# Local attention's channel sums as one-hot matmuls, and one block of scores a period as powers of e on GpSimd

## The chip, the cores and the metric

The kernel runs on one core of a Trainium2 chip. The metric is the device time of one execution in microseconds (us); of several runs the median counts. Engine names in the profile: PE is TensorE, ACT is ScalarE, DVE is VectorE, POOL is GpSimd, SP is SyncE, which here only issues DMAs.

## What is computed

Two attentions over the same input of 2,048 tokens with 512 channels, 32 heads of 16 channels each, mixed by a gate per token. Cut to what matters:

```python
S, D, H, Dh = 2048, 512, 32, 16
g = sigmoid((x * gate_w).sum(-1, keepdims=True))

# A: full attention
q, k, v = split_heads(x @ A_wqkv)
p = softmax(einsum("bhqd,bhkd->bhqk", q, k) * Dh ** -0.5)
a = merge_heads(einsum("bhqk,bhkd->bhqd", p, v)) @ A_wo

# B: local, dilated attention: 8 keys, at distances 0, 2, ..., 14
q, k, v = split_heads(x @ B_wqkv)
idx = pos[:, None] - 2 * arange(8)[None, :]          # masked where negative
logits = einsum("bhsd,bhswd->bhsw", q, k[idx]) * Dh ** -0.5
o = einsum("bhsw,bhswd->bhsd", softmax(masked(logits)), v[idx])
b = merge_heads(o) @ B_wo

return g * a + (1 - g) * b
```

All inputs and the output are bf16.

## The kernel before

**Full attention.** A *block* is the score tile of one head, 128 keys and 512 queries: 32 heads x 16 key tiles x 4 query chunks = 2,048 blocks. A *period* is one group of four heads (`i`, 0 to 7) with one query chunk (`c_`, 0 to 3); it has 64 blocks, and there are 32 periods, ordered so that two chunks run side by side through the eight groups, then the other two (the change of chunk pair comes after period 16). Four heads sit in four 32-row strips of the array. A block's scores are one matmul (`qk`, line 851), ScalarE turns them into powers of e in sets of three or two blocks (`ex`, line 857: 1,536 or 1,024 columns, tile `pT`, three buffers for each of the two sizes), and a second matmul adds their product with V into the PSUM accumulator `acc` (`pv`, line 870, `pv_mm`, line 818), which has one buffer. A 17th column of ones in V gives the sum of the powers. At a period's end VectorE transposes `acc` (`po1`, line 961, tile `accT`), which frees it for the next period, divides (`po2`) and transposes back (`po3`).

Some of the blocks don't go to ScalarE: in each period `n_dve` blocks (line 20; 3, 2, 4 or 6, in all 116) are done on VectorE by `d_group` (line 888), usually two together. There `dq` makes the scores in a `misc` PSUM tile, `p1` evicts them into `dt`, three scalar_tensor_tensor instructions (`p2`, `p3`, `p4`; tiles `dg` and `pd`, 1,024 wide for two blocks) build the bit pattern of the power, and `pv` multiplies with V. So ScalarE has 1,932 blocks.

**Local attention.** `b_tile` (line 639) runs for each of 16 tiles of 128 tokens. Q, K and V are projected on TensorE in four 32-column strips (`proj`, `mm_ct`, line 250), evicted by VectorE, and K and V written to a scratch in HBM (`kvd`). From there two DMAs load the eight shifted copies of K and V, 1 MB each (`loadk`, `loadv`; tiles `ksh`, `vsh`). GpSimd multiplies K's copies with Q and adds up the 16 channels of each head by halving adds, in two halves of four copies (`logits_half`, line 698). VectorE and ScalarE make the softmax of the 8 logits (`sm_max` to `sm_mul`, lines 723 to 744; `sm_sum` folds 1 - g, `omg`, into 1/sum), GpSimd multiplies with V's copies and adds them (`av_half`, line 749), TensorE transposes the result `obb` (`fin`, line 789) and VectorE puts it into `obt`.

**Output.** For each token tile the output projections of A (`a_mm`) and B (`b_mm`) are done on TensorE, and VectorE mixes them: `a_ev` scales A's by g (`fa`), `b_ev` adds B's (`osb`). The tiles of the last chunk do part of it ahead (`fb_ev`, `fa_ev`, `t_ev`).

**What sets the order.** Every step is an `op` with an engine, an estimated time, a due time, its dependencies, and tokens for the buffers that it takes. `list_schedule` (line 79) simulates these estimates and puts all steps into one order; `Chained` (line 231) and `chain` pin each engine's instructions to it. So each queue is fixed when the program is built, whatever happens on the chip. Where the plan sees TensorE with little to do, it inserts filler matmuls of zeros into `acc` (`zeros`, line 833), which keep TensorE's clock up. Nearly all instructions carry the line of a helper: 239 for `Chained`, 248 for `mm`; lines 422, 616 and 795 are the transpositions of x, of the gate's row, and of `obb`.

The plan's estimate for ScalarE and for the two halves of a tile's logits on GpSimd:

```python
b = op("act", 0.455 * n, ex, tn, deps=[a], alloc=[tp], use=[tr_], name=f"ex{k}")
l0 = opb("pool", 11.9, logits_half(0), tb + 8, deps=[lk, qa], alloc=[tlg], use=[tks, tqb], name=f"lg{t}")
```

Of the kernel before, what the change touches and what calls it, by code (L numbers as in the profile page):

```python
# [20 lines left out]
    dve_tiles=2,  # L21
    b_start=26.0,
# [4 lines left out]
H = 32  # L27
DH = 16
# [6 lines left out]
LN2 = 0.6931471805599453  # L35
SHIFT = 175.0
# [38 lines left out]
WAVE = lambda n: 0.2 + 0.22 * n  # L75
AHEAD = dict(pe=0.10, dve=0.12, act=0.25, pool=0.5, sp=0.0)
# [105 lines left out]
def kernel(  # L182
# [74 lines left out]

    ops = []
# [22 lines left out]
    n_dve = cfg["n_dve"]  # L281
    units, first_unit = [], []
    for pi, (c_, i) in enumerate(periods):
        dset = set(dorder[:n_dve[pi]])
        first_unit.append(len(units))
        units += [(pi, t, j) for t in range(NT) for j in range(4) if (t, j) not in dset]
# [18 lines left out]
    kv_scr = tc.dram_tile([16 + S, 2 * D], BF16, name="kv_scr")  # L305
# [3 lines left out]
    identf = const.tile([NT, NT], FP32, name="identf")  # L309
    ones_t = const.tile([128, QW], BF16, name="ones_t")  # L310
    rowc = const.tile([128, 3], FP32, name="rowc")
    z32 = const.tile([128, 32], BF16, name="z32")
    selq = const.tile([128, 128], BF16, name="selq")
# [13 lines left out]
    def init_warm():  # L327
        V.memset(z32[:], 0.0)
        V.memset(ones_t[:], 1.0)
# [32 lines left out]
    def load_x(sc):  # L362
        def s():
            if sc < 2:
                xl = work.tile([128, W, D], BF16, name="xld", tag="ksh", bufs=2)
            else:
                xl = work.tile([128, NG, QW], BF16, name="xld2", tag="oat", bufs=2)
            SP.dma_start(out=xl[:, 0:TPC, :], in_=x2d[sc * QW:(sc + 1) * QW, :].rearrange("(t p) d -> p t d", p=128))
            xld[sc] = xl
        return s  # L370
# [11 lines left out]
    def load_wo():  # L382
# [4 lines left out]
        SP.dma_start(out=kv_scr[0:16, 0:D], in_=woarr[16:32, 0, :])  # L387
        SP.dma_start(out=kv_scr[0:16, D:2 * D], in_=woarr[16:32, 1, :])

    xtok = [tok("ksh", 2), tok("ksh", 2), tok("oat", 2), tok("oat", 2)]  # L390
# [240 lines left out]
    o_kvd, o_obt = [], []  # L631
    obt_tiles, obt_tok = {}, {}
    WH = W // 2
    HB = D

    def opb(*a, **k):
        return op(*a, cls="b", **k)

    def b_tile(t):
# [3 lines left out]
        rel = max(21.0, tb - 60.0)  # L643

        def proj(key, off, c0):
            def s():
                if c0 == 0:
                    st[key] = misc_ps([128, D])
                    if key == "pk":
                        st["kvs"] = work.tile([128, 2 * D], BF16, name="kvs", tag="kvs", bufs=1)  # L650
                    if key == "pq":
                        st["qb"] = work.tile([128, D], BF16, name="qb", tag="qb", bufs=1)
                for c in range(c0, c0 + 2):
                    mm_ct(st[key], xT[:, c, t * 128:(t + 1) * 128], bw[:, c, off * D:(off + 1) * D], c == 0, c == DC - 1)
            return s
        tkv = tok("kvs", 1)

        def ke():
            V.tensor_copy(out=st["kvs"][:, 0:D], in_=st["pk"][:])

        def ve():
            V.tensor_copy(out=st["kvs"][:, D:2 * D], in_=st["pv"][:])

        def kvd():
            SP.dma_start(out=kv_scr[16 + t * 128:16 + (t + 1) * 128, :], in_=st["kvs"][:])
        tk = tok("misc", 2)
        a = opb("pe", WAVE(2), proj("pk", 1, 0), tb - 14, dense=2, deps=[o_bw] + o_xt[cb], alloc=[tk, tkv], rel=rel)
        a = opb("pe", WAVE(2), proj("pk", 1, 2), tb - 13.5, dense=2, deps=[a], use=[tk])
        ka = opb("dve", 0.71, ke, tb - 13, deps=[a], use=[tk, tkv])
        tk = tok("misc", 2)  # L670
        a = opb("pe", WAVE(2), proj("pv", 2, 0), tb - 12, dense=2, deps=[o_bw] + o_xt[cb], after=[a], alloc=[tk], rel=rel)
        a = opb("pe", WAVE(2), proj("pv", 2, 2), tb - 11.5, dense=2, deps=[a], use=[tk])
        va = opb("dve", 0.71, ve, tb - 11, deps=[a, ka], use=[tk, tkv])
        o_kvd.append(opb("sp", 0.6, kvd, tb - 10, deps=[va], use=[tkv], lat=3.0))

        tqb = tok("qb", 1)

        def qe():
            V.tensor_scalar(out=st["qb"][:], in0=st["pq"][:], scalar1=float(DH) ** -0.5, scalar2=None, op0=ALU.mult)
        tk = tok("misc", 2)  # L680
        a = opb("pe", WAVE(2), proj("pq", 0, 0), tb - 6, dense=2, deps=[o_bw] + o_xt[cb], alloc=[tk, tqb], rel=rel)
        a = opb("pe", WAVE(2), proj("pq", 0, 2), tb - 5.5, dense=2, deps=[a], use=[tk])
        qa = opb("dve", 0.71, qe, tb - 5, deps=[a], use=[tk, tqb])

        def loadk():
            base = kv_scr[16 + t * 128:16 + (t + 1) * 128, :]
            st["ksh"] = work.tile([128, W, D], BF16, name="ksh", tag="ksh", bufs=2)
            SP.dma_start(out=st["ksh"][:], in_=_ap(base, [[2 * D, 128], [-DIL * 2 * D, W], [1, D]]))

        def loadv():  # L690
            st["vsh"] = work.tile([128, W, D], BF16, name="vsh", tag="vsh", bufs=1)
            vbase = kv_scr[16 + t * 128:16 + (t + 1) * 128, D:2 * D]
            SP.dma_start(out=st["vsh"][:], in_=_ap(vbase, [[2 * D, 128], [-DIL * 2 * D, W], [1, D]]))
        tks, tvs, tlg, tob, tbb = tok("ksh", 2), tok("vsh", 1), tok("lg", 2), tok("ob", 1), tok("obb", 1)
        lk = opb("sp", 0.7, loadk, tb - 8, deps=o_kvd[max(0, t - 1):t + 1] + [o_wo], alloc=[tks], lat=10.0)
        lv = opb("sp", 0.7, loadv, tb + 10, deps=o_kvd[max(0, t - 1):t + 1] + [o_wo], alloc=[tvs], lat=9.0)

        def logits_half(hf):
            def s():
                if hf == 0:  # L700
                    st["lg"] = work.tile([128, H, W], FP32, name="lg", tag="lg", bufs=2)
                ksh, lg, qb = st["ksh"], st["lg"], st["qb"]
                prod = work.tile([128, WH, D], FP32, name="prod", tag="prod", bufs=1)
                for w_ in range(WH):
                    for c0 in range(0, D, HB):
                        G.tensor_tensor(out=prod[:, w_, c0:c0 + HB], in0=ksh[:, hf * WH + w_, c0:c0 + HB],
                                        in1=qb[:, c0:c0 + HB], op=ALU.mult)
                pv_ = prod[:].rearrange("p w (h d) -> p w h d", d=DH)
                n = DH
                while n > 2:  # L710
                    n //= 2
                    ws = min(WH, max(1, HB // (H * n)))
                    for w0 in range(0, WH, ws):
                        G.tensor_tensor(out=pv_[:, w0:w0 + ws, :, 0:n], in0=pv_[:, w0:w0 + ws, :, 0:n],
                                        in1=pv_[:, w0:w0 + ws, :, n:2 * n], op=ALU.add)
                G.tensor_tensor(out=lg[:, :, hf * WH:(hf + 1) * WH].rearrange("p h w -> p w h"),
                                in0=pv_[:, :, :, 0], in1=pv_[:, :, :, 1], op=ALU.add)
                if hf == 1 and t * 128 < DIL * (W - 1):
                    G.affine_select(out=lg[:], in_=lg[:], compare_op=ALU.is_ge, fill=NEG,
                                    base=t * 128, pattern=[[0, H], [-DIL, W]], channel_multiplier=1)  # L720
            return s

        def sm_max():
            st["mx"] = work.tile([128, H], FP32, name="mx", tag="mx", bufs=2)
            V.tensor_reduce(out=st["mx"][:], in_=st["lg"][:], axis=AX.X, op=ALU.max)

        def sm_sub():
            lg, mx = st["lg"], st["mx"]
            mx_bc = _ap(mx[:], [list(mx[:].ap[0]), [1, H], [0, W]])
            V.tensor_tensor(out=lg[:], in0=lg[:], in1=mx_bc, op=ALU.subtract)  # L730
# [4 lines left out]
        def sm_sum():  # L735
# [5 lines left out]
            V.tensor_scalar(out=rr[:], in0=rr[:], scalar1=omg[:, t:t + 1], scalar2=None, op0=ALU.mult)  # L741
            st["rr"] = rr

        def sm_mul():
            ex, rr = st["lg"], st["rr"]
            rr_bc = _ap(rr[:], [list(rr[:].ap[0]), [1, H], [0, W]])
            V.tensor_tensor(out=ex[:], in0=ex[:], in1=rr_bc, op=ALU.mult)

        def av_half(hf):
            def s():  # L750
                if hf == 0:
                    st["ob"] = work.tile([128, D], FP32, name="ob", tag="ob", bufs=1)
                else:
                    st["obb"] = work.tile([128, D], BF16, name="obb", tag="obb", bufs=1)
                vsh, attn, ob = st["vsh"], st["lg"], st["ob"]
                prod = work.tile([128, WH, D], FP32, name="prod", tag="prod", bufs=1)
                hn = HB // DH
                for w_ in range(WH):
                    for c0 in range(0, D, HB):
                        a0 = attn[:, c0 // DH:c0 // DH + hn, hf * WH + w_:hf * WH + w_ + 1]  # L760
                        attn_bc = _ap(a0, [list(a0.ap[0]), [W, hn], [0, DH]])
                        G.tensor_tensor(out=prod[:, w_, c0:c0 + HB].rearrange("p (h d) -> p h d", d=DH),
                                        in0=vsh[:, hf * WH + w_, c0:c0 + HB].rearrange("p (h d) -> p h d", d=DH),
                                        in1=attn_bc, op=ALU.mult)
                for c0 in range(0, D, HB):
# [358 lines left out]
```

## Time and profile before

| | |
|---|---|
| three runs | 930.05, 941.4, 946.99 us; median 941.4 |
| the profiled execution | 933.24 us, of it the span 931.5 us |
| granted TensorE clock, mean | 0.984 of full speed |
| first and last exponential of full attention | 21.3 and 919.4 us from the span's start |
| filler matmuls (`acc<-ones_t,z`) | 271 |
| DMA | 47.39 MB, of it 16 MB `ksh` and 16 MB `vsh` |

Times in the page are microseconds from the first to the last instruction of one profiled execution. A row names the line, the engine, the operation, the tile written and the tiles read, their shapes, and the count; behind the bar stand the busy time, the mean of one in ns, and the idle time of the engine just before, with the releaser that ended most of it. Matmuls overlap, so their mean is longer than the pace at which they follow each other.

Stages, busy us of each engine in each (TensorE, its weight loads, VectorE, ScalarE, GpSimd), then the granted clock:

```
20.00:120.00 100.00, 91.70 (x957) 31.38 (x953) 78.89 (x108) 98.00 (x89) 65.08 (x52) 1.00 0.22 65
320.00:420.00 100.00, 90.08 (x899) 30.90 (x897) 78.91 (x104) 99.32 (x90) 92.02 (x73) 1.00 0.17 49
480.00:560.00 80.00, 71.68 (x707) 21.87 (x708) 52.27 (x67) 72.66 (x66) 62.80 (x51) 0.91 0.16 52
560.00:680.00 120.00, 104.83 (x906) 33.32 (x905) 100.50 (x108) 119.75 (x108) 117.03 (x82) 1.00 0.18 51
860.00:919.00 59.00, 50.91 (x492) 16.53 (x488) 43.45 (x53) 56.43 (x51) 0.00 (x0) 1.00 0.02 6
```

### The profile page before, as it was taken

Reading aid. Unit: us, or ns where it says so; the run is one execution under the profiler, and the core shown is the slowest. Engines: PE = TensorE matmul, PEld = TensorE weight load, DVE = VectorE, ACT = ScalarE, POOL = GpSimd, SP = SyncE. Lnnn points to the kernel's source line nnn. Section 1 sums busy time; section 2 is a strip of 40 time slices with the busy share of each in tenths; the row PEclk is TensorE's granted clock in tenths of the full one; section 3 lists DMA queues with packets and bytes.
Section 4 is the critical chain, followed back from the end, with each engine's and each line's share of the span. In section 5 each row is a group of like instructions: output and inputs, shape, how many; then the busy total and the mean of one; then the engine's idle time right before and its main releaser. Section 6 shows DMA issues by size and latency. Waiting matters only on the chain.

```text
span 931.5 us, 18744 instructions
## 1 busy us (share of the span) xinstructions
PE 818.5 (88%) x7720; PEld 271.4 (29%) x7720; DVE 688.0 (74%) x873; ACT 890.5 (96%) x799; POOL 703.4 (76%) x540
## 2 busy tenths in 40 slices
PE   7999998889999989988899899888888788889887
PEld 4223232223332223322223223222222222222222
DVE  4687967858787787886336777988778667876776
ACT  4999998999999999999998989999999999999994
POOL 2357969797999699979893999999999989920000
PEclk9999999999999999999999979999999999899999
DMA  9301210303030211031301020130330100100001
GB/s 272 104 2 58 60 44 1 103 1 103 1 104 13 91 58 46 6 99 57 109 20 62 22 88 12 46 103 1 102 99 4 43 3 2 46 1 2 1 1 47
DMA packets 43934, 47.39 MB, mean 51 GB/s; under 512 B 1812, under 2 KB 41284, under 8 KB 43848
## 3 DMA queue, kind: packets, MB, share of 16 engines
q1 hardware_dynamic: 43848, 46.19, 16.0%
q8 instruction: 60, 0.98, 0.4%
q14 instruction: 26, 0.21, 0.1%
HBM read 39.86 MB, written 6.33 MB: 50 GB/s over the span
## 4 chain that ended last, share of the span: by engine, by line
ACT 58%; issue 21%; PE 14%; DVE 5%; DMA 1%; SPq 0%; DVEq 0%; ACTq 0%
ACT pT L239 57%; PE ring L248 5%; PE misc_ps L248 4%; PE acc L248 4%; DVE dg L239 2%; ACT lg L239 1%; DMA xld<-in_A_x_dram 1%; PE misc L248 1%; DVE pd L239 1%; DVE osb L239 0%; ACT xT L239 0%; DVE dt L239 0%; DVE qt L239 0%; DVE kmax_all L239 0%; PE pxt L422 0%
## 5 line engine op out<-in xcount | busy, mean ns | idle before, releaser
L239 ACT ACTIVATE pT<-ring 128x1536 bf16<-128x1536 f32 (+1 forms) x773 | 880.4, 1367 | 17.2 <-PE ring L248 9.8
L248 PE MATMUL ring<-qt,kt_all 32*128 32x512 bf16 x1932 | 309.3, 385 | 91.6 <-ACT pT L239 86.5
L248 PE MATMUL acc<-pT,vp_all 128*17 128x512 bf16 (+1 forms) x1932 | 317.1, 390 | 1.8 <-DVE accT L239 1.5
L239 POOL TENSOR_TENSOR prod<-prod 128x512 f32<-128x512 f32 (+1 forms) x208 | 284.0, 1377 | 6.3
L239 POOL TENSOR_TENSOR prod<-ksh,qb 128x512 f32<-128x512 bf16 x128 | 177.5, 1416 | 86.2 <-DVE absq L239 29.7
L248 PEld LDWEIGHTS <-kt_all 32*128 32x128 bf16 x2048 | 116.5, 91 | 391.3 <-issue 384.2
L239 POOL TENSOR_TENSOR prod<-vsh,lg 128x512 f32<-128x512 bf16 x128 | 163.6, 1307 | 20.2 <-DVE lg L239 15.9
L239 DVE TENSOR_SCALAR dt<-misc 128x512 f32<-128x512 f32 x116 | 79.5, 686 | 64.7 <-PE misc L248 63.2
L248 PEld LDWEIGHTS <-vp_all 128*17 128x17 bf16 (+1 forms) x1932 | 69.7, 88 | 132.9 <-issue 124.3
L239 DVE SCALAR_TENSOR_TENSOR dg<-dt,dg 128x1024 bf16<-128x1024 uint16 x65 | 106.3, 1636 | 1.6
L239 DVE SCALAR_TENSOR_TENSOR pd<-dg,dt 128x1024 uint16<-128x1024 bf16 x65 | 100.5, 1546 | 6.9 <-PE acc L248 5.7
L248 PE MATMUL misc_ps<-xT,wst 128*32 128x512 bf16 x1024 | 98.2, 390 | 1.0 <-ACT kt_all L239 0.8
L239 DVE SCALAR_TENSOR_TENSOR dg<-dt 128x1024 bf16<-128x1024 uint16 x65 | 93.8, 1443 | 1.8
L248 PE MATMUL acc<-ones_t,z 128*32 128x512 bf16 x271 | 95.1, 390 | 0.0
L248 PE MATMUL misc_ps<-bw,xT 128*32 128x512 bf16 x768 | 71.8, 385 | 0.6 <-DVE kvs L239 0.6
L248 PE MATMUL misc<-qt,kt_all 32*128 32x512 bf16 x116 | 44.7, 386 | 0.2 <-DVE dt L239 0.2
L248 PE MATMUL misc_ps<-woarr,oat 128*32 128x512 bf16 x512 | 42.6, 382 | 0.6 <-DVE osb L239 0.6
L248 PEld LDWEIGHTS <-xT 128*32 128x32 bf16 (+1 forms) x1088 | 33.6, 96 | 25.4 <-issue 18.1
L239 DVE STREAM_TRANSPOSE accT<-acc 128x512 f32<-128x512 f32 x32 | 22.8, 712 | 17.3 <-PE acc L248 17.1
L239 DVE TENSOR_SCALAR kt_all<-misc_ps,rowc 128x512 bf16<-128x512 f32 x28 | 22.5, 802 | 17.3 <-PE misc_ps L248 17.3
L239 DVE TENSOR_TENSOR qt<-qt,misc_ps 128x512 bf16<-128x512 bf16 x32 | 21.8, 682 | 17.3 <-PE misc_ps L248 17.1
L248 PE MATMUL acc<-pd,vd_all 128*17 128x512 bf16 x116 | 29.1, 388 | 5.3 <-DVE pd L239 2.9
(72 smaller groups left out, 534.1 us busy)
## 6 DMA issues: line engine op xcount, KB each, us to landing
ksh<-kv_scr SPq DMA_DIRECT2D x16, 1024.0 KB, 5.7
vsh<-kv_scr SPq DMA_DIRECT2D x16, 1024.0 KB, 5.6
kv_scr<-kvs SPq DMA_DIRECT2D x16, 256.0 KB, 2.1
xld<-in_A_x_dram SPq DMA_DIRECT2D x4, 512.0 KB, 5.3
out_dram<-osb SPq DMA_DIRECT2D x16, 128.0 KB, 1.7
wst<-in_A_wqkv_dram SPq DMA_DIRECT2D x3, 512.0 KB, 5.3
bw<-in_B_wqkv_dram SPq DMA_DIRECT2D x1, 1536.0 KB, 11.6
bwo<-in_B_wo_dram SPq DMA_DIRECT2D x1, 512.0 KB, 13.8
```

What stands on the lines that cost most here:

```text
L239: return chain_on(key, f(*a, **k))
L248: return chain(nc.tensor.matmul(out, lhsT=lhsT, rhs=rhs, start=start, stop=stop, **kw))
```

## The change

Two things are changed, and what hangs on them.

1. **One block a period as powers on GpSimd.** `n_pow = (1,) * 32` takes one further block of each period from ScalarE (so 1,900 remain there). `pow_block` makes its scores in a `misc` tile, VectorE evicts them scaled into `xg` (SBUF, since GpSimd doesn't read PSUM here), GpSimd computes e to the power of `xg` with tensor_tensor and `ALU.pow`, in four pieces of 128 columns, and TensorE multiplies the result `pg` with V. `n_dve` stays.
2. **Channel sums on TensorE.** K and Q of local attention are projected transposed, channels on partitions (`projT`), so that a shifted copy of K is a window along the token axis: `kTb` holds 128 tokens and 16 before them, which `halo` copies from the tile before. GpSimd multiplies window and Q (`prods`, two instructions a step), and the sums over a head's 16 channels are fp32 matmuls with the one-hot matrix `hsel` (`sums`, steps of eight), whose result VectorE evicts (`le`, tile `lT`) and TensorE transposes back (`turn`). The max and the subtraction read the logits from PSUM. K no longer goes through HBM: `ksh` and its load are gone, the scratch holds V alone.
3. The multiplication by 1/sum (`sm_mul`) moves from VectorE to GpSimd, and 1 - g moves from the softmax into the eviction of B's output projection (`b_ev`, `fb_ev`). `av_half` becomes three steps a half (`avs` twice, `ava`), and `prod` gets two buffers.

The order of all queues is made anew by `list_schedule`. GpSimd's steps of one tile now stand mixed with those of the next, with the four power pieces between them.

```diff
+    n_pow=(1,) * 32,
+EULER = 2.718281828459045
+PT2, TMUL = 0.6, 1.43
+POW = 6.5
...
+    gorder = [(NT - 1 - NTD, j) for j in range(4)]
+    n_pow = cfg["n_pow"]
...
-        dset = set(dorder[:n_dve[pi]])
+        dset = set(dorder[:n_dve[pi]]) | set(gorder[:n_pow[pi]])
...
+        def projT(key, off, c0):
...
+                for c in range(c0, c0 + 2):
+                    for d_ in range(DC):
+                        mm(st[key][:, c, :], bw[:, d_, off * D + c * 128:off * D + (c + 1) * 128], xT[:, d_, ts], d_ == 0, d_ == DC - 1)
...
+        def halo():
+            if t == 0:
+                G.memset(kT_tiles[t][:, :, 0:PAD], 0.0)
+            else:
+                G.tensor_copy(out=kT_tiles[t][:, :, 0:PAD], in_=kT_tiles[t - 1][:, :, 128:128 + PAD])
...
+                for w_ in range(w0, w1):
+                    b0 = PAD - DIL * (hf * WH + w_)
+                    G.tensor_tensor(out=st["prod", hf][:, w_], in0=kT_tiles[t][:, :, b0:b0 + 128], in1=st["qT"][:], op=ALU.mult)
...
+                for w_ in range(w0, w1):
+                    for c in range(DC):
+                        mm(st["pl", hf][32 * c:32 * c + 32, :], hsel[:, w_].rearrange("p h w -> p (h w)"),
+                           st["prod", hf][:, w_, c, :], w_ == 0, w_ == WH - 1, tile_position=(0, 32 * c))
...
+            for hf in range(2):
+                chain(nc.tensor.transpose(out=st["pt"][:, hf, :], in_=st["lT"][:, hf, :], identity=identf[:]))
...
-            V.tensor_tensor(out=ex[:], in0=ex[:], in1=rr_bc, op=ALU.mult)
+            G.tensor_tensor(out=ex[:], in0=ex[:], in1=rr_bc, op=ALU.mult)
...
+    def pow_block(pi, t, j, lo, hi):
...
+        tx, te, tp = tok("misc", 2), tok("xg", 2), tok("pg", 1)
...
+        def p1():
+            st["xg"] = work.tile([128, QW], FP32, name="xg", tag="xg", bufs=2)
+            V.tensor_scalar(out=st["xg"][:], in0=st["x"][:], scalar1=float(DH) ** -0.5, scalar2=None, op0=ALU.mult)
+
+        def pw():
+            st["pg"] = work.tile([128, QW], BF16, name="pg", tag="pg", bufs=1)
+            for q_ in range(0, QW, 128):
+                G.tensor_tensor(out=st["pg"][:, q_:q_ + 128], in0=_ap(e_t[:], [list(e_t[:].ap[0]), [0, 128]]),
+                                in1=st["xg"][:, q_:q_ + 128], op=ALU.pow)
...
+        a = op("pool", POW, pw, lo + 12.0, deps=[a], alloc=[tp], use=[te], lat=POW + 3.0, name=f"pow{pi}")
+        o_pv[pi].append(op("pe", 0.25, pv, hi, dense=1, deps=[a, o_t0[pi], o_v[(4 * i + j, t)]], use=[tp, acc_tok[pi]], name=f"gpv{pi}"))
...
-                V.tensor_tensor(out=st["o"], in0=st["pb"][:], in1=st["fa"], op=ALU.add)
+                V.scalar_tensor_tensor(out=st["o"], in0=st["pb"][:], scalar=omg[:, t:t + 1], in1=st["fa"],
+                                       op0=ALU.mult, op1=ALU.add)
```

## The prediction

> **What bounds the kernel now.** I read the page first, from the engines' shares to the chain of waits.
>
> ```profile
> PE 818.5 (88%) x7720; PEld 271.4 (29%) x7720; DVE 688.0 (74%) x873; ACT 890.5 (96%) x799; POOL 703.4 (76%) x540
> ACT 58%; issue 21%; PE 14%; DVE 5%; DMA 1%; SPq 0%; DVEq 0%; ACTq 0%
> L239 ACT ACTIVATE pT<-ring 128x1536 bf16<-128x1536 f32 (+1 forms) x773 | 880.4, 1367 | 17.2 <-PE ring L248 9.8
> L248 PE MATMUL ring<-qt,kt_all 32*128 32x512 bf16 x1932 | 309.3, 385 | 91.6 <-ACT pT L239 86.5
> ```
>
> ScalarE's exponentials are the bound: 1,932 blocks take 880.4 us, 0.4557 us a block, with 17.2 us of idle among them. TensorE's score matmuls wait 91.6 us in all, nearly all for ScalarE: that is TensorE's spare time. Next the waits, to see what starves ScalarE:
>
> ```profile
> ACT pT L239 <- PE ring L248: 9.8, 16, 1.6
> ACT pT L239 <- PE acc L248: 6.7, 5, 2.9
> ```
>
> 9.8 us because scores came late, 6.7 us because an accumulator (`acc`) was freed late, so that PV matmuls stopped and the pT buffers ran full. The longest of these (2.9 us) is at the change of chunk pair, near 511 us; the timeline of VectorE there:
>
> ```profile
> 504.06 1.21 DVE L239 SCALAR_TENSOR_TENSOR pd<-dg,dt 128x1024 uint16<-128x1024 bf16 x1
> 508.58 0.69 DVE L239 TENSOR_SCALAR qb<-misc_ps 128x512 bf16<-128x512 f32 x1 [3.31 <-PE misc_ps L248]
> 509.49 0.69 DVE L239 TENSOR_TENSOR osb<-misc_ps,fa 128x512 bf16<-128x512 f32 x1 [0.22 <-PE misc_ps L248]
> 510.10 0.71 DVE L239 STREAM_TRANSPOSE accT<-acc 128x512 f32<-128x512 f32 x1
> ```
>
> The transposition that frees `acc` stands behind `qb` and `osb`. Last, GpSimd by kinds of operation:
>
> ```profile
> L239 POOL TENSOR_TENSOR prod<-prod 128x512 f32<-128x512 f32 x176 | 254.7, 1461 | 3.8
> L239 POOL TENSOR_TENSOR prod<-ksh,qb 128x512 f32<-128x512 bf16 x128 | 177.5, 1416 | 86.2 <-DVE absq L239 29.7 <-issue 29.6 <-DVE qb L239 14.0
> L239 POOL TENSOR_TENSOR prod<-vsh,lg 128x512 f32<-128x512 bf16 x128 | 163.6, 1307 | 20.2 <-DVE lg L239 15.9 <-DVE dg L239 1.5 <-DVE qt L239 0.5
> L239 POOL TENSOR_TENSOR prod<-prod 128x256 f32<-128x256 f32 x32 | 29.3, 915 | 2.5
> L239 POOL TENSOR_TENSOR ob<-prod 128x512 f32<-128x512 f32 x16 | 28.1, 1757 | 1.3
> L239 POOL TENSOR_TENSOR obb<-ob,prod 128x512 bf16<-128x512 f32 x16 | 24.2, 1512 | 1.3
> L239 POOL TENSOR_TENSOR lg<-prod 128x128 f32<-128x128 f32 x32 | 20.0, 624 | 2.5
> ```
>
> 697.4 us of tensor_tensor, done by 822 us. `obb` is written at 105.2 us for the first tile and at 819.5 us for the last, so a tile takes 714.3 / 15 = 47.6 us.
>
> **ScalarE.** 32 blocks leave: 32 x 0.4557 = **14.6 us**, on the bound. Nothing else changes there (16 small exponentials stay).
>
> **GpSimd.** Gone: per half tile three adds of 512 elements, one of 256 and one of 128, the channel sums. Left by rows: 177.5 + 163.6 + (176 - 96) x 1.461 = 116.9 + 28.1 + 24.2; new are 16 multiplications by 1/sum (256 elements, row 0.915) = 14.6 and 15 halo copies, about 0.3 each: 529 us, 33.1 a tile. On top come 32 powers at P each. No row shows a power. From below: four adds of 128 elements, 4 x 0.624 = 2.5 us. From above no row is near; a power made of ten such adds would be 25 us. I take the 6.5 us that the changed kernel's plan writes for it, because the plan's other constants agree with rows: 0.455 us a block (0.4557), 11.9 for half a tile's logits (4 x 1.416 + 3 x 1.461 + 0.915 + 0.624 = 11.6), 1.43 a product (1.416). Then GpSimd has 529 + 208 = 737 us, against 697: it fits, and lies beside ScalarE at no cost. The cover ends where a tile and its 47.6 / 27.6 = 1.72 powers fill the tile's time: (47.6 - 33.1) / 1.72 = 8.4 us; with waits in between I say 8.
>
> **New waits.** TensorE's queue is in order, and now waits for GpSimd at 32 sums and 32 power blocks, where it did so at 16 transpositions of `obb`. Behind each stand the score matmuls that feed ScalarE. With P as planned they are ready first (the plan keeps 3 us after each power): nothing. On SP's queue 16 loads of 1 MB (`ksh`) vanish and the scratch writes halve; GpSimd waited 11.1 us for `ksh` in all, off the bound: nothing. On VectorE come 32 evictions `xg` (0.686, the row of `dt`) = 22, 32 of `lT` (between 0.1 and the 0.417 of `obt`, I take 0.3) = 10; 16 x (0.60 + 0.47) = 17 go. 688 becomes about 703 us, 76%: hidden as a sum, not in its order (below).
>
> **TensorE.** Added per tile: four steps of eight fp32 matmuls of 128 columns, and two fp32 transpositions. The only fp32 row is one tiny transposition, 0.133 us of weight load and 0.229 of matmul. For a step, from below eight 128-column matmuls at bf16's pace, 0.2 us; from above, in the built program each fp32 matmul is two loads and two matmuls, so 16 x 0.36 = 5.8 us if none overlap. I take the row that also has four column strips side by side, eight bf16 matmuls of 512 columns in 0.61 us. A tile: 4 x 0.61 + 2 x 0.36 = 3.2, in all 51 us. The Trainium skill, FP8 and Floating Point Precision, section TensorE Precision Notes, says that true fp32 takes four passes through the array. By it 128 columns cost as much as 512, an estimate that leaves the sum as it is; no row here has an fp32 matmul with sums. The K and Q projections turn from 16 strips of 512 columns into 16 full matmuls of 128, about the same. 71 filler matmuls go (271 to 200), at about 0.22 us start to start 15 us. Net 36 of the 91.6 us to spare. Taking idle as inverse to spare time, the 9.8 us of late scores become 9.8 x 91.6 / 55.6 = 16.1: **+6.3** (0 to 15).
>
> **VectorE's order.** At the change of chunk pair the changed order puts between the last `osb` and the transposition of `acc`: `dt`, the three 1024-wide steps, `fa`: 0.69 + 3 x 1.22 + 0.74 = 5.1 us where `qb` and `osb` took 1.4. ScalarE is already starved there, so **+3.7** (1 to 6). In the last five periods VectorE keeps its six blocks and gets `xg`, while a period of ScalarE is shorter by 0.46: **+1.5** at the end (0 to 4).
>
> A rule against this change: VectorE's three-operand steps slow down while GpSimd works.
>
> ```profile
> L239 DVE SCALAR_TENSOR_TENSOR dg<-dt,dg 128x1024 bf16<-128x1024 uint16 x14 | 28.9, 2065 | 0.5
> L239 DVE SCALAR_TENSOR_TENSOR dg<-dt,dg 128x1024 bf16<-128x1024 uint16 x8 | 9.8, 1221 | 0.1
> ```
>
> The first is 600 to 780 us, GpSimd busy; the second 830 to 900, GpSimd idle. After 822 us only two or three powers are left, 20 us at most, so I add nothing. The Trainium skill, SBUF — State Buffer, section Who interferes with whom, says that one of the two holds the shared port for its whole instruction. By it a power in one piece would hold VectorE for the whole 6.5 us, in four for 1.6, near the 1.4 of a product; the sum would stay.
>
> **Sum.** -14.6 + 6.3 + 3.7 + 1.5 = -3.1 us. The profiled execution took 933.24 us (span 931.5, 1.7 around it): 930.1. It lies 0.87% under the median of the runs shown, 941.4 (930.05 to 946.99); scaled by 1.0087, **938.3 us**.
>
> **Rivals.**
> - *The whole gain stays.* ScalarE's share speaks for it, and early matmuls may absorb the new waits: 933.2 - 14.6 = 918.6, scaled 926.6; if 4 us of today's 17.2 idle go too, 922.6. Against it: 91.6 us of spare time is little for a program whose queues are fixed. 0.14.
> - *Powers are dearer than their slot.* From P = 8 us GpSimd becomes the bound while local attention runs, some 28 powers, and TensorE waits behind each: 28 x (P - 8). P = 9 gives 930.1 + 28 = 958, scaled 966; P = 13 gives 1,070, scaled 1,080. For it: no row, and a slot with 20% of room. Against it: the plan's constants are true elsewhere. 0.17. This is the slower side.
> - *The fp32 sums overlap badly.* At twice my price TensorE needs 102 - 15 = 87 of its 91.6 us: by the same rule idle would explode; I put 30 us on it, 960, scaled 968. Decides from about 1 us a step. 0.10.
> - *The change does what it says?* 32 blocks leave ScalarE in any case, in all 760 activations instead of 773. Something unseen: 0.04.
>
> **Numbers.** The forecast has 0.55: its bounds (-14.6 + 1 to -14.6 + 25) are 919.6 to 943.6, scaled 927.6 to 951.9. About 2% (18.8 us, 922.6 and 960.2) is what a measurement of this kernel can tell from no change. Faster: a third of the first rival and run-to-run spread, 0.09. Slower: most of the second and third and some unseen, 0.28. The same: 0.63. The range 920 to 965 leaves out 0.05 below and 0.15 above (P over 9, sums at twice the price).
>
> **What would show it.** ScalarE's blocks near 865.8 us; its idle 25 to 30 us instead of 17, the longest wait, for `acc`, near 510 us; four power pieces of about 1.6 us; GpSimd near 737 us; eight fp32 sums in 0.6 us. A power of over 8 us, a step over 1 us, or ScalarE's idle under 18 us would make it wrong.

## The result, and the profile after

The changed kernel takes 3,238.5 us (median of four runs, 3,238.0 to 3,242.0) beside 943.2 us for the kernel before (930.05 to 946.99): 3.456 times as long, 95% interval 3.435 to 3.477. Ratios here and below leave out runs in the slower of a kernel's two states, so they differ a little from the quotient of the two medians. The forecast of 938.3 us and its whole range are missed by a factor of more than three.

The page of the changed kernel: the engines' busy time, the chain that ended last, and four groups of instructions (busy us and mean ns of one behind the bar, then the idle time before them).

```profile
PE 947.4 (29%) x8705; PEld 311.1 (10%) x8705; DVE 640.3 (20%) x913; ACT 892.3 (28%) x786; POOL 3119.6 (96%) x540
POOL 89%; issue 5%; PE 4%; DVE 1%; ACT 1%; POOLq 1%; ACTq 0%
L243 POOL TENSOR_TENSOR pg<-e_t,xg 128x128 bf16<-128x128 f32 x128 | 2653.1, 20747 | 44.2 <-DVE xg L243 44.2
L243 ACT ACTIVATE pT<-ring 128x1536 bf16<-128x1536 f32 x760 | 881.8, 1281 | 2318.8 <-PE ring L252 1955.4
L252 PE MATMUL acc<-pg,vp_all 128*17 128x512 bf16 x32 | 18.6, 580 | 1918.2 <-POOL pg L243 1918.2
L252 PE MATMUL misc_ps<-prod,hsel 128*32 128x128 f32 x1024 | 45.5, 294 | 142.3 <-POOL prod L243 142.2
```

The bound has moved from ScalarE (96% busy before, 28% now) to GpSimd (76% before, 96% now). ScalarE's exponentials still cost 881.8 us; what is new is 2,318.8 us of idle before them. The third line is the reason: one piece of 128 columns takes 20.7 us where 1.6 us had been forecast, four of them 82.9 us. Read the idle columns as a relay: ScalarE waits for scores (1,955.4 us), the scores wait on TensorE's queue, and TensorE waits for GpSimd's power in front of 32 PV matmuls (1,918.2 us). Every row of the page names a releaser; following the largest number from row to row leads to the cause.

One period in the timeline (start, duration, engine and group, in brackets the idle time before it and its releaser):

```profile
127.28 82.88 POOL L243 TENSOR_TENSOR pg<-e_t,xg 128x128 bf16<-128x128 f32 x4 [1.21 <-DVE xg L243]
131.31 7.03 ACT L243 ACTIVATE pT<-ring 128x1536 bf16<-128x1536 f32 x6
135.40 1.22 DVE L243 SCALAR_TENSOR_TENSOR dg<-dt,dg 128x1024 bf16<-128x1024 uint16 x1
136.73 0.39 PE L252 MATMUL acc<-pT,vp_all 128*17 128x512 bf16 x2
210.21 0.58 PE L252 MATMUL acc<-pg,vp_all 128*17 128x512 bf16 x1 [73.09 <-POOL pg L243]
211.44 1.45 ACT L243 ACTIVATE pT<-ring 128x1536 bf16<-128x1536 f32 x1 [73.10 <-PE ring L252]
```

The power starts at 127.28. TensorE goes on to 137.1, some 10 us, because the plan put the PV matmul of `pg` that far down its queue; then it stands for 73.09 us, and ScalarE, one step behind, for 73.10. Nothing behind that matmul in TensorE's queue may pass it, so the score matmuls of the next blocks wait too, although they need nothing from GpSimd. Busy time by stretch (length, then TensorE, weight loads, VectorE, ScalarE, GpSimd, the granted clock):

```profile
112.00:138.00 26.00, 24.33 (x257) 8.69 (x256) 20.25 (x34) 25.53 (x24) 18.15 (x8) 0.99 0.01 2
138.00:210.00 72.00, 0.00 (x0) 0.00 (x0) 3.47 (x7) 0.34 (x1) 72.00 (x4) 0.51 0.00 0
```

In the first stretch TensorE and ScalarE are busy nearly throughout, as before. In the second, 72 us long, GpSimd works throughout, TensorE not at all, and VectorE and ScalarE for 3.8 us together.

### The profile page after: what moved, and what is told of

It is laid out like the page before. It is cut to its first block, busy times and chain, and to the rows that moved or that the text cites. A ratio compares the mean times of both kernels' runs of the same rounds, so it can differ in the third digit from the quotient of the medians.

```text
span 3236.2 us, 20765 instructions
## 1 busy us (share of the span) xinstructions
PE 947.4 (29%) x8705; PEld 311.1 (10%) x8705; DVE 640.3 (20%) x913; ACT 892.3 (28%) x786; POOL 3119.6 (96%) x540
## 4 chain that ended last, share of the span: by engine, by line
POOL 89%; issue 5%; PE 4%; DVE 1%; ACT 1%; POOLq 1%; ACTq 0%
POOL pg L243 78%; POOL prod L243 9%; PE acc L252 1%; PE misc_ps L252 1%; PE ring L252 1%; ACT pT L243 1%; POOLq L1220 1%; POOL ob L243 1%; POOL obb L243 0%; DVE dg L243 0%; POOL lg L243 0%; DVE osb L243 0%; POOL woarr L243 0%; PE misc L252 0%; DVE pd L243 0%
## 5 line engine op out<-in xcount | busy, mean ns | idle before, releaser
L243 POOL TENSOR_TENSOR pg<-e_t,xg 128x128 bf16<-128x128 f32 x128 | 2653.1, 20747 | 44.2 <-DVE xg L243 44.2
L243 ACT ACTIVATE pT<-ring 128x1536 bf16<-128x1536 f32 x760 | 881.8, 1281 | 2318.8 <-PE ring L252 1955.4
L252 PE MATMUL acc<-pg,vp_all 128*17 128x512 bf16 x32 | 18.6, 580 | 1918.2 <-POOL pg L243 1918.2
L252 PE MATMUL ring<-qt,kt_all 32*128 32x512 bf16 x1900 | 344.0, 429 | 48.8 <-ACT pT L243 44.2
L243 POOL TENSOR_TENSOR prod<-kTb,qTb 128x512 f32<-128x512 bf16 x128 | 151.1, 1202 | 20.9 <-DVE qTb L243 15.1
L243 POOL TENSOR_TENSOR prod<-prod 128x512 f32<-128x512 f32 x80 | 106.4, 1345 | 1.3
L243 DVE TENSOR_SCALAR xg<-misc 128x512 f32<-128x512 f32 x32 | 21.7, 678 | 424.1 <-PE ring L252 347.3
L252 PE MATMUL misc_ps<-prod,hsel 128*32 128x128 f32 x1024 | 45.5, 294 | 142.3 <-POOL prod L243 142.2
L243 DVE SCALAR_TENSOR_TENSOR dg<-dt,dg 128x1024 bf16<-128x1024 uint16 x65 | 82.5, 1270 | 1.7
L252 PE MATMUL misc<-qt,kt_all 32*128 32x512 bf16 x148 | 63.6, 443 | 0.0
## 6 DMA issues: line engine op xcount, KB each, us to landing
woarr<-in_A_wo_dram SPq DMA_DIRECT2D x4, 128.0 KB, 11.8
```

What stands on the lines that cost most here:

```text
L243: return chain_on(key, f(*a, **k))
L252: return chain(nc.tensor.matmul(out, lhsT=lhsT, rhs=rhs, start=start, stop=stop, **kw))
```

## The experiments

The questions: is it the power alone, or do the sums on TensorE lose as well? Why does a power cost 82.9 us? Does it hurt through GpSimd's total time (throughput) or through the wait that it puts into TensorE's queue (latency)? And would the forecast have held at the price that it assumed?

**The sums alone.** No power blocks, so ScalarE has its 1,932 blocks again.

```diff
-    n_pow=(1,) * 32,
+    n_pow=(0,) * 32,
```

> The change without its powers: no block goes to GpSimd (n_pow all 0), ScalarE has its 1,932 blocks again, the channel sums stay on TensorE. Theory (the powers are the whole loss: 128 pieces of 20.7 us): GpSimd about 470 us busy, and the time within 2% of before, 930 to 955 us. Rival (the fp32 sums and TensorE's new waits for GpSimd cost much of their own): over 965 us.

931.7 us (10 runs) beside 937.8 (13 runs): ratio 0.9962, interval 0.9922 to 1.0003. To see whether that is a gain, the same kernel ran again on another chip:

> The kernel of e1_sums_only again (the channel sums on TensorE, no power), for a closer ratio: 0.9962 [0.9922, 1.0003] so far. If the sums on TensorE are a gain of their own, the interval now lies below 1; if they are neutral, it holds 1 or its middle moves to within 0.2% of it.

930.6 us (12 runs) beside 937.1 (23 runs): 0.9966, interval 0.9937 to 0.9995. This interval lies just below 1: the kernel with the channel sums on TensorE is about 0.3% faster, and it is the fastest version of the study. The gain comes with the clock. Among the 23 runs of the kernel before, the time follows TensorE's granted clock, from 928.5 us at 0.992 to 948.9 us at 0.961; the twelve runs of the sums alone lie along the same line, 927.6 us at 0.998 to 939.4 us at 0.974, and have on average 0.990 where the others have 0.978. Why their clock is higher isn't shown. The powers are the whole loss. The engines' busy time in the first of these two runs:

```profile
PE 837.4 (90%) x8716; PEld 312.4 (34%) x8716; DVE 656.4 (71%) x881; ACT 890.5 (96%) x799; POOL 525.5 (57%) x412
```

And its waits (us in all, times, longest):

```profile
ACT pT L243 <- PE acc L252: 7.8, 8, 2.0
ACT pT L243 <- PE ring L252: 6.2, 12, 1.6
```

GpSimd falls from 703 to 525.5 us (about 470 were expected), and ScalarE's waits are as short as before (9.8 for scores and 6.7 for `acc` then). But GpSimd was off the bound already, which is why 178 us less of it bring so little.

**One piece in place of four.**

```diff
-            for q_ in range(0, QW, 128):
-                G.tensor_tensor(out=st["pg"][:, q_:q_ + 128], in0=_ap(e_t[:], [list(e_t[:].ap[0]), [0, 128]]),
-                                in1=st["xg"][:, q_:q_ + 128], op=ALU.pow)
+            G.tensor_tensor(out=st["pg"][:], in0=_ap(e_t[:], [list(e_t[:].ap[0]), [0, QW]]),
+                            in1=st["xg"][:], op=ALU.pow)
```

> The changed kernel with each block's power as one instruction of 512 columns. Theory (a power costs by the column, 20.7 us / 128 = 162 ns): 83 us a block, the time again about 3,240 us. Rival (20.7 us is a fixed cost of an instruction, paid four times because of the pieces): about 21 us a block, GpSimd 465 + 32 x 21 = 1,130 us, the time 1,150 to 1,250 us.

3,212.5 us (one run). The group on GpSimd:

```profile
L243 POOL TENSOR_TENSOR pg<-e_t,xg 128x512 bf16<-128x512 f32 x32 | 2626.7, 82086 | 42.3 <-DVE xg L243 42.3
```

82.1 us for 512 columns in one instruction, 4 x 20.7 = 82.9 in four. The pieces are not the cost; the columns are.

**The power by itself.** A kernel that leaves both attentions out and runs nothing but powers and products on an idle GpSimd, with other operands, types, widths and numbers of partitions:

```python
g("g_pow128", 128, bc(e_t, 128), xs[:, 0:128])        # e to the power of x, e repeated
g("g_powdense", 128, ed[:, 0:128], xs[:, 0:128])      # e as a full tile
g("g_powzero", 128, bc(e_t, 128), zero[:, 0:128])     # exponent 0
g("g_square", 128, xpos[:, 0:128], bc(two, 128))      # x to the power of 2
for p in (1, 8, 16, 32, 64):                          # fewer partitions
    g(f"g_powp{p}_", 32, bc(e_t, 32, p), xs[0:p, 0:32], p=p)
```

> Powers alone on GpSimd, one instruction after the other, with nothing else on the chip but copies of x to the output (attention is left out altogether). Sizes 16, 32, 128 and 512 columns; base as one repeated column or as a full tile; output fp32 or bf16, exponents fp32 or bf16; exponents 0, 1, small, large and about -30; base 2; squares; 1 to 128 partitions. Theory (a software loop by the column): 16, 32, 128, 512 columns take 2.6, 5.2, 20.7 and 83 us whatever the types, the base or the load of other engines. Rival a (a special operand makes it slow: the repeated column, the bf16 output or values outside a fast range): one of these variants takes a few us for 128 columns. Rival b (the port is shared with a busy VectorE): alone, 128 columns take far less than 20.7 us.

```profile
L64 POOL TENSOR_TENSOR g_pow<-e_t,xs 128x512 bf16<-128x512 f32 x1 | 81.9, 81908 | 0.0
L64 POOL TENSOR_TENSOR g_powdense<-ed,xs 128x128 bf16<-128x128 f32 x1 | 20.8, 20764 | 0.0
...
L64 POOL TENSOR_TENSOR g_square<-xpos,two 128x128 bf16<-128x128 f32 x1 | 20.7, 20708 | 0.0
...
L64 POOL TENSOR_TENSOR g_powp__163<-e_t,xs 1x32 bf16<-1x32 f32 x1 | 5.4, 5405 | 0.0
...
L64 POOL TENSOR_TENSOR g_pow<-e_t,xs 128x16 bf16<-128x16 f32 x1 | 2.9, 2894 | 0.0
L64 POOL TENSOR_TENSOR g_mult<-e_t,xs 128x512 bf16<-128x512 f32 x1 | 1.0, 1032 | 0.0
```

The price is the instruction's own: 81.9 us alone and 82.1 at the same width in the kernel, so contention adds next to nothing. Between 16 and 512 columns it is (81,908 - 2,894) / 496 = 159 ns a column, the same for a square as for an exponential, and the same for one partition as for 128 (5.4 us for 32 columns on either). A product of the same shape takes 1.03 us: the power is 79 times dearer.

**Throughput or latency: four powers.** The plan is told the true price, and only four periods have a power, so that GpSimd's total fits easily.

```diff
-    n_pow=(1,) * 32,
+    n_pow=(0, 0, 0, 1, 0, 0, 0, 0, 0, 0, 1, 0, 0, 0, 0, 0, 0, 1, 0, 0, 0, 0, 0, 0, 1, 0, 0, 0, 0, 0, 0, 0),
-POW = 6.5
+POW = 82.9
```

> Four power blocks instead of 32 (periods 4, 11, 18 and 25), and the plan told the price that the chip showed, 82.9 us, in place of 6.5. GpSimd then has 525 + 4 x 83 = 857 us of work in 930. Theory (not GpSimd's sum but the time until one block's power is there counts: the accumulator has one buffer, its period lasts 28 us, and it can't be freed before a power that takes 83 us): each power still holds everything for 50 to 70 us, the time 1,130 to 1,220 us. Rival (GpSimd's sum is the bound, so four powers fit into its idle time): 925 to 950 us.

1,149.9 us (one run), some 218 us above the kernel with the sums alone, 55 for each power, although GpSimd's sum fits (835.3 us busy in a span of 1,148.1). Its waits:

```profile
ACT pT L243 <- PE acc L252: 216.3, 17, 66.0
...
PE acc L252 <- POOL pg L243: 146.5, 4, 55.2
```

Four waits of TensorE for `pg`, and as many long ones of ScalarE (25 to 66 us), with short ones 216.3 us: nearly the whole loss. Even a plan that knows the price can't hide it: a period lasts 28 us, `acc` has one buffer, and it can't be emptied before the product of a power of 83 us has been added. The next period can't begin to add, the `pT` buffers run full, and ScalarE stops. So latency alone is enough to do the harm.

**A power in every second period**, as the changed kernel otherwise is.

```diff
-    n_pow=(1,) * 32,
+    n_pow=(1, 0) * 16,
```

> A power block in every second period (16), the plan as in the changed kernel. Theory (each power holds the accumulator's period for about 70 us, since the next period's local attention can't run on GpSimd either): 931 + 16 x 70 = 2,050 us, 1,980 to 2,120. Rival (the sum of GpSimd's work): 16 x 83 + 470 and the 140 us of waits and ends of the changed kernel = 1,940 us or less.

2,068.5 us (one run), inside the theory's range and above the rival's 1,940: (2,068.5 - 931.7) / 16 = 71 us for each power. With one in every period, in one piece, it is (3,212.5 - 931.7) / 32 = 71.3 us. The loss for each power is the same with 16 and with 32.

```profile
PE 887.4 (43%) x8721; PEld 311.9 (15%) x8721; DVE 639.1 (31%) x897; ACT 891.4 (43%) x793; POOL 1817.5 (88%) x476
```

This is the run that parts the two accounts. With a power in every period GpSimd is busy for 3,119.6 of 3,236.2 us, so a full GpSimd would explain that time as well as the wait does. With 16 powers it is idle for 249 us; its 1,817.5 us and the 117 us of idle of the changed kernel would end at 1,934, and the span is 133 us longer.

**The forecast's own price.** Five products of 512 columns in place of the power, 6.6 us a block, which is what the plan and the forecast assumed. These products are not powers of e, so the full attention's result differs; waits and queues are those of the change.

```diff
-            for q_ in range(0, QW, 128):
-                G.tensor_tensor(out=st["pg"][:, q_:q_ + 128], in0=_ap(e_t[:], [list(e_t[:].ap[0]), [0, 128]]),
-                                in1=st["xg"][:, q_:q_ + 128], op=ALU.pow)
+            for _ in range(5):
+                G.tensor_tensor(out=st["pg"][:], in0=_ap(e_t[:], [list(e_t[:].ap[0]), [0, QW]]),
+                                in1=st["xg"][:], op=ALU.mult)
```

> The changed kernel in its own order, but each power block is five plain multiplications of 512 columns in place of four power pieces (the block's exponentials are left out, so the output isn't the reference's); that is 5 x 1.2 to 1.4 = 6 to 7 us, the 6.5 us that the plan allots. Theory (only the price of a power was wrong in the prediction's sum): a ratio to before of 0.985 to 1.01, ScalarE's pT group about 866 us, the longest waits for acc near 510 us. Rival (a fixed queue order that waits for GpSimd at 64 places loses by itself): a ratio over 1.02.

951.6 us (4 runs): ratio 1.0149, interval 1.0080 to 1.0217. The engines' busy time and the exponentials on the page of this kernel:

```profile
PE 862.7 (91%) x8705; PEld 307.2 (32%) x8705; DVE 700.6 (74%) x913; ACT 881.3 (93%) x786; POOL 727.1 (76%) x572
L243 ACT ACTIVATE pT<-ring 128x1536 bf16<-128x1536 f32 x760 | 870.7, 1313 | 45.2 <-PE ring L252 30.0
```

Its waits:

```profile
ACT pT L243 <- PE ring L252: 30.0, 44, 2.7
ACT pT L243 <- PE acc L252: 12.5, 7, 6.6
```

So at the assumed price the change would have been 1.5% slower, not 0.3% faster. That lies between the two answers that the expectation gave, above the theory's 1.01 and below the rival's 1.02. The profiled run, of 953.2 us, had the lowest granted clock of the four, 0.918 where the others had 0.962 to 0.978. ScalarE saves 880.4 - 870.7 = 9.7 us against the kernel before and gives it back three times over: its idle grows from 17.2 to 45.2 us, most of it scores that come late. The longest wait is where the forecast put it, at the change of chunk pair. VectorE and ScalarE there:

```profile
517.36 0.68 DVE L243 TENSOR_SCALAR dt<-misc 128x512 f32<-128x512 f32 x1
518.08 1.96 DVE L243 SCALAR_TENSOR_TENSOR dg<-dt 128x1024 bf16<-128x1024 uint16 x1
520.07 2.01 DVE L243 SCALAR_TENSOR_TENSOR dg<-dt,dg 128x1024 bf16<-128x1024 uint16 x1
522.11 2.00 DVE L243 SCALAR_TENSOR_TENSOR pd<-dg,dt 128x1024 uint16<-128x1024 bf16 x1
524.04 0.74 DVE L243 TENSOR_SCALAR fa<-misc_ps,g_sp 128x512 f32<-128x512 f32 x1
524.70 0.70 DVE L243 STREAM_TRANSPOSE accT<-acc 128x512 f32<-128x512 f32 x1
525.95 6.88 ACT L243 ACTIVATE pT<-ring 128x1024 bf16<-128x1024 f32 x6 [6.57 <-PE acc L252]
```

`accT` stands behind `dt`, three steps of 2 us and `fa`, and ScalarE waits 6.57 us.

**Taking that wait away.** The two blocks that VectorE does ahead of `accT` there are dropped, so that ScalarE has two blocks more.

```diff
-    n_dve=(3,) * 14 + (2,) * 4 + (4,) * 9 + (6,) * 5,
+    n_dve=(3,) * 14 + (2, 2, 0, 2) + (4,) * 9 + (6,) * 5,
```

> As the run with five multiplications, but with no VectorE blocks in period 17 (two more for ScalarE), so that the three 1,024-wide steps no longer stand before the transposition that frees the accumulator at the change of chunk pair. Theory (that place costs 3.7 to 6.6 us, the rest of the loss is TensorE's): the wait of 6.6 us near 526 us is gone, the time 3 to 6 us shorter than that run, a ratio to before near 1.01. Rival (the time moves to the next wait): no change.

950.9 us (4 runs), ratio 1.0153, interval 1.0046 to 1.0260: no gain is seen, though four runs between 945.9 and 958.1 us don't exclude the 3 us of the theory's lower end. On the page the wait is gone (the longest for `acc` is now 3.3 us, 8.5 in all after 12.5), but the waits for scores rise from 30.0 to 34.8 us, and all idle before the exponentials is 45.3 us where it was 45.2. A longest wait is not yet a price.

**A cheap block.** One product in place of the five, so that the block's scores, eviction and PV matmul stay and GpSimd's part nearly vanishes.

> As the run with five multiplications for a power, but with one (512 columns, 1.0 to 1.4 us; the exponentials of the block are left out). Theory (the loss of 1.5% there comes from the order and from TensorE, not from GpSimd's time): within 0.5% of that run, a ratio to before of 1.005 to 1.02. Rival (GpSimd's 6.6 us a block is what TensorE waits for): a ratio of 0.985 to 1.0.

942.5 us: ratio 1.0047, interval 1.0001 to 1.0093. One of its ten runs took 2,215 us and is left out of the ratio. It is the run that was profiled: TensorE is busy for 2,205 of its 2,213 us, a score matmul takes 861 ns where the next run of this kernel has 386, and VectorE and GpSimd are no busier than there (644.5 and 505.4 us, beside 688.3 and 577.0). What slowed TensorE isn't shown. The kernel ran again:

> The kernel of e7_cheap_mult again, one product of 512 columns in place of the power (its output is not a power of e), for its profile and a closer ratio. If the 1.5% of the five products comes with GpSimd's time, this one is at most 0.5% above the kernel before and ScalarE's waits for scores are nearer to the 6 us of the kernel with the sums alone than to 30. If it comes with the steps that TensorE and VectorE get (scores into misc, eviction, PV), the ratio is 1.010 to 1.015 and the waits are 25 to 30 us.

943.0 us (12 runs): ratio 1.0091, interval 1.0055 to 1.0127. This falls between the two answers that the expectation set apart. ScalarE's exponentials on this kernel's page:

```profile
L243 ACT ACTIVATE pT<-ring 128x1536 bf16<-128x1536 f32 x760 | 869.0, 1323 | 34.5 <-PE ring L252 20.5
```

The same group on the page of the sums alone, second run, on the same chip, and below it the group of the fp32 sums, which is used further down:

```profile
L243 ACT ACTIVATE pT<-ring 128x1536 bf16<-128x1536 f32 (+1 forms) x773 | 881.8, 1334 | 20.9 <-PE ring L252 11.6
...
L252 PE MATMUL misc_ps<-prod,hsel 128*32 128x128 f32 x1024 | 42.3, 277 | 0.6 <-DVE kt_all L243 0.3
```

869.0 + 34.5 = 903.5 and 881.8 + 20.9 = 902.7: all that ScalarE saves comes back as idle, with GpSimd at 1.1 us a block. That page of the sums alone is of its slowest run, 939.4 us; the first run's page, of 930.5 us, has 880.5 + 15.1 = 895.6, so more than the saving comes back, and the medians are 12 us apart. So a further block a period off ScalarE was worth nothing here, even at a price near nothing on GpSimd. Why the scores then come late isn't shown: TensorE and VectorE each get more steps and another order, and TensorE's granted clock is lower as well (on average 0.974 in these twelve runs, 0.990 in those of the sums alone). No run parted these three. How much of the five products' 1.5% is GpSimd's time is not settled: the interval of this kernel (0.55 to 1.27%) and that of the five products (0.80 to 2.17%) overlap.

**The price in steps.** Part of the columns real powers, the rest products (no powers of e there), to find where the cover ends and how the loss grows.

```diff
+            for a_, b_, op_ in ((0, 64, ALU.pow), (64, QW, ALU.mult)):
+                G.tensor_tensor(out=st["pg"][:, a_:b_], in0=_ap(e_t[:], [list(e_t[:].ap[0]), [0, b_ - a_]]),
+                                in1=st["xg"][:, a_:b_], op=op_)
```

> Of each power block 64 columns are a real power and 448 a product (those 448 columns are not powers of e, so the output differs). By the prices measured so far a block should take about 10.6 + 0.95 = 11.5 us on GpSimd, GpSimd's sum 525 + 32 x 11.5 = 893 us. From the runs with 16 and 32 powers, a power of 82.9 us costs 71 to 72 us, so some 11 us of each lie beside other work. Theory A (what counts is how long the one power block holds up TensorE beyond a fixed cover of about 11 us): at the edge, 945 to 975 us. Theory B (the rival of the prediction, 28 x (P - 8)): 930 + 28 x 3.5 = 1,028, scaled 1,037. Theory C (only GpSimd's sum counts, it fits into the span): like the five products, 945 to 958.

1,007.6 us (4 runs), ratio 1.0767, interval 1.0707 to 1.0827: above theory A, below B, and C is refuted. The engines' busy time and the chain that ended last:

```profile
PE 883.4 (88%) x8705; PEld 309.2 (31%) x8705; DVE 669.2 (67%) x913; ACT 884.9 (88%) x786; POOL 870.5 (87%) x476
POOL 54%; ACT 16%; PE 15%; issue 9%; DVE 6%; DMA 1%; SPq 0%; POOLq 0%; ACTq 0%; DVEq 0%
```

And the waits:

```profile
ACT pT L243 <- PE ring L252: 75.1, 69, 10.6
PE misc_ps L860 <- POOL obb L243: 21.8, 8, 10.6
PE acc L252 <- POOL pg L243: 13.7, 6, 3.3
```

TensorE waits longest, 10.6 us at once, not for the power but for `obb`, a step of local attention that now comes late on GpSimd. GpSimd's 870.5 us fit into the span as a sum, but from 400 to 500 us it has one pause, of 1.6 us, and its steps are 54% of the chain that ended last. This fits the throughput rival, at work while local attention runs.

With 128 columns of powers:

> Of each power block 128 columns are a real power and 384 a product (those 384 are not powers of e). Price of a block about 20.75 + 0.85 = 21.6 us, GpSimd's sum 525 + 691 = 1,216 us. Theory A (32 x (P - 11) on top of about 932): 932 + 339 = 1,271, range 1,240 to 1,310. Theory B (28 x (P - 8)): 930 + 381 = 1,311, scaled 1,322. Theory C (GpSimd's sum and 30 us at the start and 100 us at the end): 1,216 to 1,250 at most if local attention's own steps fill all the rest.

1,281.5 us (2 runs), ratio 1.370, interval 1.359 to 1.381: within A's range, with B's 1,311 above it and C's 1,250 below. C isn't refuted by that: it had put GpSimd's sum at 1,216 us, the page shows 1,162.3, and with the 117 us of idle of the changed kernel this makes 1,279. TensorE's waits for `pg` have taken over:

```profile
ACT pT L243 <- PE ring L252: 305.9, 113, 17.1
PE acc L252 <- POOL pg L243: 218.2, 27, 13.8
```

The steps together. The price is the mean GpSimd time of a block from each kernel's own row; the loss per block is the time less that of the sums alone on the same chip, over 32.

| a block on GpSimd | price, us | time, us | loss per block, us | price less loss |
|---|---|---|---|---|
| one product | 1.12 | 943.0 | 0.39 | 0.7 |
| five products | 6.63 | 951.6 | 0.62 | 6.0 |
| 64 columns of powers | 11.8 | 1,007.6 | 2.41 | 9.4 |
| 128 columns of powers | 21.7 | 1,281.5 | 10.97 | 10.7 |
| 512 columns, one piece | 82.1 | 3,212.5 | 71.3 | 10.8 |

In the lower rows the last column is the cover. It levels off at 10.7 us, close to the 10 us that the timeline shows between a power's start and TensorE's stop. These rows alone don't tell the wait from a full GpSimd, which is busy for 91% and 96% of the span in the last two; the runs with 16 and with four powers do. From 128 to 512 columns each microsecond of price costs a microsecond in every period. There is no sharp corner: at 11.8 us, one microsecond beyond the cover, the loss is already 2.4.

## Why the prediction was wrong

**The step that failed: GpSimd, "I take the 6.5 us that the changed kernel's plan writes for it".** The reason given was that the plan's other constants agree with rows. But those belong to operations that the kernel before runs and that have rows to compare with; this one belongs to an operation without a row. 0.455 us for a block on ScalarE says nothing about a power on GpSimd. It measured 82.9 us, 12.8 times the value taken. The upper bound, "a power made of ten such adds", 25 us, was no bound: it rested on a guess of how a power is made. The lower bound of 2.5 us misses by 33 times. And an unknown whose upper end at 25 us would, by the rival's own formula, have added 28 x 17 = 476 us should never have left the range at 965.

**The slower rival had the direction and nearly the law.** "Powers are dearer than their slot", 28 x (P - 8): with the measured P it gives 930 + 28 x 74.9 = 3,027 us. The mechanism it named, GpSimd as the bound while local attention runs, with TensorE waiting behind each power, is what 64 columns point to, and with a power in every period GpSimd is nearly full at the true price too (96%). But the loss doesn't need a full GpSimd. The fuller account is the fixed place of a matmul in an in-order queue: the loss comes out alike with 16 and with 32 powers if all are counted, not 28, the cover is 10.7 us, not 8, and four powers do the harm with GpSimd's total well within the span. Its examples ended at P = 13.

**New waits, "nothing".** This held only "with P as planned", as the text said. With the five products TensorE's waits name `pg` for 1.4 us of weight loads in all; with the power it is 1,918.2 us ahead of the PV matmuls alone.

**ScalarE, -14.6 us.** 9.7 us in the kernel at the assumed price (870.7 after 880.4); the blocks that remain took 870.7 / 1,900 = 0.4583 us, not 0.4557. The direction holds, a third of the size is lost.

**TensorE's sums.** Right: 64 steps of eight fp32 matmuls took 42.3 us of TensorE's time in the sums-alone kernel of the second chip, 0.66 us a step against 0.61. Its row counts 1,024 instructions, 16 a step, since each fp32 matmul is two. TensorE as a whole rose by 847.4 - 818.5 = 29 us there and by 19 in the first run of that kernel, with 36 predicted for the whole change. The rival of badly overlapping sums falls with this.

**Late scores, +6.3 us.** Mis-sized, and assigned to the wrong part. With the sums alone the waits for scores were 6.2 and 11.6 us in two profiles after 9.8 before: no clear growth. With the five products they were 30.0 us, +20.2 where +6.3 was predicted (0 to 15 as the bounds). TensorE's wait ahead of its score matmuls, the spare time of the sum, was 54.5 us there, nearly the 55.6 predicted; so it was the rule that failed, idle taken as inverse to spare time.

**VectorE's order, +3.7 us (1 to 6).** The place and the cause are as predicted; with five products the wait is 6.57 us, 3.7 more than the 2.9 of before. But in the reordered kernel, where that wait is gone, ScalarE's idle as a whole is no shorter. VectorE's busy time, 703 predicted, is 700.6; GpSimd's, 737 predicted, is 727.1.

**The tail, +1.5 us (0 to 4).** From the start of the last exponential to the end: 951.4 - 935.8 = 15.6 us with five products, 931.5 - 918.4 = 13.1 before, so +2.5.

At the assumed price, then, the terms give -9.7 of ScalarE's work, +28.0 of its idle and +2.5 of tail, 20.8 us, and the spans differ by 951.4 - 931.5 = 19.9. So even there the forecast's sum would have been too low: -3.1 us, where the five products measured +1.5%, though that is still within 2% of no change.

**The shared port.** The prediction added nothing for it, and weighed the Trainium skill, SBUF — State Buffer, section Who interferes with whom. That section says that a VectorE instruction with two SBUF inputs contends with a GpSimd instruction that reads SBUF. The power reads SBUF, and yet VectorE's step at 135.40, in the middle of a piece of 20.7 us, took 1.22 us, which is its time on an idle GpSimd (1.221 us before). Beside plain products the same steps took 2.0 us (2.065 us as a mean in the kernel before, 2.01 us with the five products at 520.07). For powers the rule isn't seen here.

## What to carry to other kernels

An operation that has no row has no price: a plan's constant for it is a claim, and before work is moved onto it, time it alone, at the width that is meant, on the engine that is meant. A long instruction on a side engine is not hidden because that engine's sum fits; what counts is how far behind it, in an in-order queue, the first instruction stands that needs its result, here about 10 us. And once scores come late, a block taken off the busiest engine can return as that engine's idle time, as it did here, so compare busy plus idle, not busy time.

## What the runs showed of the hardware

- A power on GpSimd costs 159 ns a column, for every base and exponent that was tried, for fp32 and bf16 exponents alike, and however few partitions it covers: 5.4 us for 32 columns on one partition, on 64 and on 128. A product takes 1.03 us for 512 columns.
- TensorE's granted clock falls while TensorE stands: 0.51 in the 72 us without a matmul, 0.99 in the 26 us ahead of them, 0.63 as the mean of the span. The first PV matmul after the pause takes 0.58 us where the ones ahead of it took 0.39.
